# Hourglass attention plus token mixing on one core: query and key loaded as six rows on each of 96 partitions, value halves swapped while cast, four-quadrant products, explicit PSUM slots

## The chip, the cores and the metric

The kernel runs on one core of one Trainium2 chip. The metric is the device time of the whole kernel in microseconds (us), as the median of several runs. Medians and ranges that I quote are of all runs. Engines in the profile: PE is TensorE (matmul), PEld its weight loads, DVE VectorE, ACT ScalarE, POOL GpSimd, SPq the queue from which SyncE issues DMAs.

## The reference

```python
# q, k, v: (8, 8, 576, 64) = batch, heads, tokens, head width; float32
q_d, k_d, v_d = means over 4 consecutive tokens            # 144 coarse tokens
out_d     = softmax(q_d k_d^T / 8) v_d, each row repeated 4 times
out_local = softmax(q k^T / 8 where |i - j| < 4) v         # banded
x = (out_up + out_local) as (8, 576, 512)
wq, wk = x @ w_q, x @ w_k                                  # 512 x 64
mixed  = (wq wk^T / 8) @ x                                 # over tokens, no softmax
out    = relu(mixed) @ w_out                               # 512 x 512
```

## The kernel before

All eight batches run through a software pipeline: an ordered list of stages, with batches one or two apart interleaved. The helper `_InOrder` keeps every engine's instructions in program order. `...` marks cuts.

```python
def load_qk(b):
    q32 = big.tile([128, H, 4 * D], FP32, ...)      # 4 tokens on each of 128 partitions
    ...                                             # k32 alike
    r32 = big.tile([128, H, D], FP32, ...)          # the 64 tokens that remain, of q and of k
    for src, t in ((q[b], q32), (k[b], k32)):
        sp.dma_start(t, _ap(src, 0, [[4 * D, 128], [S * D, H], [1, 4 * D]]))       # 1024-byte pieces
    for i, src in enumerate((q[b], k[b])):
        sp.dma_start(r32[64 * i:64 * i + 64], _ap(src, 512 * D, [[D, 64], [S * D, H], [1, D]]))  # 256-byte pieces
def load_v(b):
    ...                                             # 10 loads, each 64 tokens on 64 partitions
    for n in range(NW):                             # 5 pairs of windows
        for c in range(2):
            sp.dma_start(v32[64 * c:64 * c + 64, n], _ap(v[b], K0[2 * n + c] * D, [[D, 64], [S * D, H], [1, D]]))
...
# casts of batch b > 0, all on GpSimd
pool.tensor_copy(...)                               # q, k, remainder
pool.tensor_copy(v16[:, :, :, 0:64], v32)           # values, one instruction of 2560 elements
...
def rem():                                          # transposed remainder to the end of qT and kT
    for i, t_ in enumerate((qT, kT)):
        evac("rem", t_[:, :, 512:S], _ap(pr, 64 * i, [[row(pr), 128], [128, NP], [1, 64]]))   # contiguous, VectorE
def sums():                                         # coarse q, k: GpSimd adds; for batch 0 the keys on VectorE
    add = (dve if i == 1 and b == 0 else pool).tensor_tensor
    ...
def av(n):                                          # value product of window pair n: two of four quadrants
    for s_ in range(2):
        for hh in range(NP):
            for c in range(2):
                h = 4 * (s_ ^ c) + hh
                pe.matmul(p_[64 * c:64 * c + 64, h // 4, 65 * hh:65 * hh + 65],
                          E[64 * c:64 * c + 64, h % 2, i, h // 2, :], v16[64 * c:64 * c + 64, n, h, :],
                          start=True, stop=True, tile_position=(64 * c, 64 * c))
def m2():                                           # second mixing product: seven matmuls of full width
    pe.matmul(p_, w_[NW][0:112], g["od"][0][0:112], start=True, stop=False)
    pe.matmul(p_, w_[NW + 1], g["od"][1], start=False, stop=False)
    for n in range(NW):
        pe.matmul(p_, w_[n], x[n], start=False, stop=(n == NW - 1))
    evac("M2", M2[0:64], p_[0:64], scale=s_mix)
def ol():                                           # output of the last 64 tokens, once per batch
    for r in range(4):
        pe.matmul(p_, rmx[:, r * S + 512:r * S + 640], wo16[:, r, :], start=(r == 0), stop=(r == 3))
```

The softmax here doesn't subtract the row's maximum and nothing guards it: scores larger than these inputs give would overflow.

## Time and profile before

| | before |
|---|---|
| time, median of 3 runs | 193.49 us (193.43 to 193.9) |
| span in the profile | 192.7 us |
| one batch in the steady part | 19.3 us |
| TensorE busy per batch | 18.5 us |
| first scores / first value product | 23.4 / 28.2 us |

The page of the profile gives busy time of each engine and then the span in 40 slices of 4.8 us: busy tenths, the granted TensorE clock, the busy share of the DMA engines, and what they moved.

```profile
PE 155.5 (81%) x2720; PEld 104.0 (54%) x2720; DVE 114.8 (60%) x286; ACT 110.7 (57%) x140; POOL 107.7 (56%) x122
...
PE   0034448885899989998999899989998999898790
...
PEclk9999555999789999999999999999999999999997
DMA  5999999899899799967999899969996943004215
GB/s 175 314 187 215 348 290 162 191 354 175 175 319 218 174 264 294 263 137 201 278 323 156 184 280 346 187 154 296 330 215 154 300 146 112 3 3 153 93 57 188
```

The next view cuts the steady part at the start of the token product (`pw`), once per batch. Its columns are the stretch, its length, each engine's busy time, the granted clock, the share of time that the DMA engines were busy, and GB/s.

```profile
core 0: us, PE busy (x) PEld busy (x) DVE busy (x) ACT busy (x) POOL busy (x), PEclk, DMA share, GB/s
62.36:81.66 19.30, 18.52 (x343) 12.43 (x341) 12.32 (x29) 13.23 (x18) 13.59 (x13) 1.00 0.95 247
81.66:100.96 19.30, 18.52 (x343) 12.43 (x341) 12.32 (x29) 13.17 (x18) 13.58 (x13) 1.00 0.87 234
```

TensorE is busy 96% of a batch at full clock. The DMA engines are busy 87 to 95% of it as well. The chain that ended last agrees with TensorE: this line gives its shares by engine.

```profile
PE 68%; DVE 17%; ACT 7%; issue 4%; POOL 2%; ACTq 0%; DVEq 0%
```

In the start, the same chain in order of time (start, length, what) shows the key sums of the first batch on VectorE, 9 us long:

```profile
18.22 1.37 DVE sum_296 L27
19.61 5.71 DVE kd_127 L27 x4
25.32 1.88 DVE kdt_129 L27
27.20 0.68 DVE vblk_201 L27 x2
```

Two groups of instructions are the remainder copies, and one batch's value cast. Columns: line, engine, operation, out and in, shapes, count, busy us and mean ns, idle time before them.

```profile
L27 DVE COPY qT<-pr 128x256 f16<-128x256 f16 x8 | 2.3, 292 | 5.1 <-PE pr L27 5.1
L27 POOL CAST v_1_149<-v_255 128x2560 f16<-128x2560 f32 x1 | 2.3, 2323 | 8.6 <-DMA v_255<-in_v_dram 8.6
```

### The profile page before, as it was taken

The page shows a single profiled execution, that of the slowest core. Times are in us where ns is not written, and L with a number is a line of the kernel's source. Part 1 is how long each engine was busy: PE and PEld are TensorE (multiplying, and loading weights), DVE is VectorE, ACT ScalarE, POOL GpSimd, SP SyncE. Part 2 cuts the span into 40 slices and gives each one's busy share as a digit, 9 for nine tenths or more (in the row PEclk, how much of TensorE's full clock was granted, in tenths as well). Part 3 has the DMA queues.
Part 4 walks back from the last instruction along what each step waited for, and adds up shares of the span by engine and source line. Part 5 has one row for each costly group of instructions (what it writes and reads, how often), then busy time and mean ns, then how long its engine had stood idle before and what let it go on. Part 6 is the DMA issues. An engine that isn't in the chain of part 4 may idle for free.

```text
span 192.7 us, 6374 instructions
## 1 busy us (share of the span) xinstructions
PE 155.5 (81%) x2720; PEld 104.0 (54%) x2720; DVE 114.8 (60%) x286; ACT 110.7 (57%) x140; POOL 107.7 (56%) x122
## 2 busy tenths in 40 slices
PE   0034448885899989998999899989998999898790
PEld 0034227853576647664776476647764776465330
DVE  6263978754646566656665666566656665685220
ACT  2037134954565767576757675767576757633422
POOL 5701991099748991895479547954895476000000
PEclk9999555999789999999999999999999999999997
DMA  5999999899899799967999899969996943004215
GB/s 175 314 187 215 348 290 162 191 354 175 175 319 218 174 264 294 263 137 201 278 323 156 184 280 346 187 154 296 330 215 154 300 146 112 3 3 153 93 57 188
DMA packets 74027, 40.54 MB, mean 210 GB/s; under 512 B 52432, under 2 KB 68880, under 8 KB 74000
## 3 DMA queue, kind: packets, MB, share of 16 engines
q1 hardware_dynamic: 73920, 40.12, 81.7%
q8 instruction: 21, 0.34, 0.7%
q14 instruction: 6, 0.05, 0.1%
q10 hardware_dynamic: 80, 0.03, 0.1%
HBM read 30.67 MB, written 9.44 MB: 208 GB/s over the span
## 4 chain that ended last, share of the span: by engine, by line
PE 68%; DVE 17%; ACT 7%; issue 4%; POOL 2%; ACTq 0%; DVEq 0%
PE po L27 15%; PE psc L27 6%; PE pav L27 5%; PE pw L27 4%; PE px L27 4%; PE pca L27 4%; PE pol L27 4%; DVE kd_127 L27 3%; PE pv L27 2%; PE pcs L27 2%; ACT kT L27 2%; PE pod L27 2%; DVE rz L27 1%; PE pws L27 1%; PE pwd L27 1%
## 5 line engine op out<-in xcount | busy, mean ns | idle before, releaser
L27 ACT COPY os<-po 128x1024 f32<-128x1024 f32 x16 | 16.2, 1012 | 14.7 <-issue 8.3
L27 DVE RECIPROCAL rz<-pav 128x8 f32<-128x8 f32 x40 | 8.1, 204 | 13.4 <-PE pav L27 13.4
L27 PE MATMUL po<-wo_91,rmx_227 128*128 128x512 f16 x64 | 15.3, 379 | 0.6 <-ACT rmx_227 L27 0.6
L27 PE MATMUL po<-wo_91,rmx_212 128*128 128x512 f16 x64 | 15.1, 379 | 0.0
L27 DVE COPY xT<-px 128x928 f16<-128x928 f16 (+1 forms) x32 | 13.8, 451 | 0.6
L27 PE MATMUL pq_236<-id_67,q_229 128*128 128x128 f16 x16 | 1.9, 312 | 12.6 <-DVE q_229 L27 12.6
L27 PE MATMUL psc<-id_67,neg 64*128 64x232 f16 (+1 forms) x80 | 9.4, 278 | 2.8 <-DVE vblk_201 L27 2.8
L27 PEld LDWEIGHTS <-rmx_227 128*128 128x128 f16 x80 | 7.2, 98 | 8.1 <-ACT rmx_227 L27 0.7
L27 PE MATMUL psc<-qT,kT 64*64 64x58 f16 (+1 forms) x640 | 11.4, 198 | 0.0
L27 PEld LDWEIGHTS <-rmx_212 128*128 128x128 f16 x80 | 7.2, 98 | 6.6
L27 DVE RECIPROCAL rc<-pca 128x8 f32<-128x8 f32 (+1 forms) x16 | 3.4, 211 | 11.8 <-PE pca L27 11.8
L27 PEld LDWEIGHTS <-wqk_90 128*128 128x128 f16 x96 | 8.3, 98 | 3.7 <-issue 0.9
L27 PEld LDWEIGHTS <-kT 64*64 64x64 f16 x640 | 8.7, 113 | 2.1 <-issue 2.1
L27 ACT COPY odT<-pod 128x448 f16<-128x448 f16 (+1 forms) x16 | 5.6, 402 | 6.3 <-PE pod L27 6.3
L27 PE MATMUL pw<-xT,wqk_90 128*128 128x288 f16 x64 | 9.2, 286 | 0.0
L27 PEld LDWEIGHTS <-q_229 128*128 128x128 f16 x16 | 1.6, 146 | 12.6 <-DVE q_229 L27 12.6
L27 POOL CAST v_0_147<-v_79 128x2560 f16<-128x2560 f32 x1 | 3.1, 3129 | 9.3 <-DMA w_92<-in_moe_w_k_dram 9.3
L27 DVE TENSOR_TENSOR wT_219<-pw,wTd 128x576 f16<-128x576 f32 x4 | 3.0, 758 | 8.6 <-ACT wTd L27 8.6
L27 DVE COPY ol<-pol 64x512 f32<-64x512 f32 x8 | 5.5, 682 | 4.3 <-PE pol L27 4.3
L27 DVE TENSOR_TENSOR wT_204<-pw,wTd 128x576 f16<-128x576 f32 x4 | 3.0, 758 | 8.0 <-ACT wTd L27 6.6
L27 DVE TENSOR_SCALAR rmx_227<-pmx 128x1024 f16<-128x1024 f32 x4 | 4.9, 1224 | 4.1 <-PE pmx L27 4.1
L27 POOL CAST v_1_149<-v_255 128x2560 f16<-128x2560 f32 x1 | 2.3, 2323 | 8.6 <-DMA v_255<-in_v_dram 8.6
(542 smaller groups left out, 540.9 us busy)
## 6 DMA issues: line engine op xcount, KB each, us to landing
out_dram<-os SPq DMA_DIRECT2D x16, 512.0 KB, 4.4
v_79<-in_v_dram SPq DMA_DIRECT2D x10, 128.0 KB, 4.6
v_255<-in_v_dram SPq DMA_DIRECT2D x10, 128.0 KB, 5.4
v_583<-in_v_dram SPq DMA_DIRECT2D x10, 128.0 KB, 3.5
v_1024<-in_v_dram SPq DMA_DIRECT2D x10, 128.0 KB, 4.4
v_1497<-in_v_dram SPq DMA_DIRECT2D x10, 128.0 KB, 3.6
v_1970<-in_v_dram SPq DMA_DIRECT2D x10, 128.0 KB, 4.3
v_2443<-in_v_dram SPq DMA_DIRECT2D x10, 128.0 KB, 3.4
```

The costliest lines, as they stand in the source:

```text
L27: return lambda *a, **k: self._tc.keep_in_program_order(f_(*a, **k))
```

## The change

Its intent: fewer and larger DMA pieces and no remainder loads; less TensorE work; value casts off GpSimd; a shorter start. Cut to its core:

```diff
-    q32, k32: [128, H, 4 * D] + r32: [128, H, D]; two loads of 1024-byte pieces, two of 256-byte pieces
+    t = big.tile([96, H, 6 * D], FP32, tag="in32", bufs=3)
+    sp.dma_start(t[:, lo:hi], _ap((q, k)[i][b], lo * S * D, [[6 * D, 96], [S * D, hi - lo], [1, 6 * D]]))
     ... (ten value loads as before, but issued one by one between other stages)

-    pool.tensor_copy(v16[:, :, :, 0:64], v32)
+    evac("va", v16[:, :, 0:4, 0:64], v32[:, :, 0:4])                       # VectorE for b > 0
+    for c in range(2):                                                     # heads 4..7: halves swapped
+        evac("vb%d" % c, v16[64 - 64 * c:128 - 64 * c, :, 4:8, 0:64], v32[64 * c:64 * c + 64, :, 4:8])

-    evac("rem", t_[:, :, 512:S], ...)                                      # 64 tokens, contiguous
+    evac("rem", t_.rearrange("p j (t f) -> p j t f", f=6)[:, :, :, 5], ...)  # 96 tokens, every sixth column

     value product (av):
-    h = 4 * (s_ ^ c) + hh
-    ... tile_position=(64 * c, 64 * c)
+    h, o = 4 * s_ + hh, 64 * (c ^ s_)
+    ... tile_position=(o, 64 * c)

     second mixing product (m2):
-    7 matmuls into p_[128 rows], one after the other
+    for i, (w_, x_) in enumerate(l_):
+        c = i % 2
+        pe.matmul(p_[64 * c:64 * c + 64], w_, x_, ..., tile_position=(0, 64 * c))
+    act.copy(half, p_[64:128])
+    dve.tensor_tensor(M2[0:64], p_[0:64], half, op=ALU.add)

+    the last 64 tokens of two batches share one output product (rest)
+    first batch: loads and casts in halves, q and k casts on ScalarE, coarse sums on TensorE (sums0)
+    constants are set between stages of the first batch instead of ahead of them
-    ps2 = tile_pool(bufs=3, PSUM); ps1 = tile_pool(bufs=2, PSUM)
+    free = {2: [0, 1, 2], 1: [3, 4]}                                       # slots given out explicitly
+    new order lists FIRST and ORDER
```

## The prediction

> **What bounds it now.** Between 43 and 160 us the kernel repeats every 19.3 us, once per batch (table of busy time by stage). TensorE is busy 18.5 of 19.3 us at full granted clock; ScalarE 13.2, VectorE 12.3, GpSimd 13.6, DMA share 0.72-0.97. The chain of waits is mostly TensorE (68% of the span), so TensorE's program order is the limit. Three costs surround it: a start of about 20 us before the repeated pattern (first scores at 23.4 us, but VectorE holds the chain to 27.9 us with the key sums: 1.37 + 5.71 + 1.88 us, and the query cast starts at 11.5 us behind constants); a granted clock of 0.66-0.68 from 20 to 41 us; and a last batch of 16.4 us after its token product starts.
>
> **What changes per batch on TensorE** (lengths from start to start in the timeline):
> - The value product uses two of four quadrants: 16 products in 0.37 us, while 32 score products on four quadrants take 0.38 us. Four-quadrant order should bring it to about 0.20 us; five windows save 0.85 us. [...]
> - The second mixing product: 7 x 0.23 = 1.62 us becomes four column pairs, about 0.87 us; saves 0.75.
> - The 64 remaining output rows: 0.86 us once per two batches; saves 0.43.
> - Transposes: 36 of 128 columns become 48 of 96, equal columns; about nothing. Split masks +0.05.
> - TensorE waits of some 0.8 us (0.4 before the mixing product, 0.2-0.3 before coarse products): new order and explicit PSUM slots perhaps halve them.
>
> Together 19.3 becomes about 16.9 us, nearly all on the critical path: 8 x 2.4 = 19 us.
>
> **What moves.** GpSimd loses the 2.3 us value cast and 0.6 us remainder cast, pays 2 x 2.85 instead of 2 x 1.9 us for query and key casts (96 partitions, 1.5 times the elements): about 12.8 us. VectorE gets the value cast, three pieces of about 0.75 us (the first 2048-element query cast took 1.19 us there), +0.65 for the halves' sum, loses 1.2 for a relu and 0.7 for the small output: about 14.3. ScalarE about 14.3. [...] Nothing should exceed TensorE, though all come near 85%.
>
> **DMA.** 1024 remainder pieces of 256 bytes per batch and two issues of about 1.5 us disappear, pieces grow from 1024 to 1536 bytes. Estimated from rates in the trace (about 180 GB/s on value loads, 400 on long pieces): about 17 us per batch becomes 16. Just under TensorE.
>
> **Start.** Split half-loads, casts on ScalarE, sums on TensorE, constants deferred: the VectorE key sums leave the chain. Batches 0 and 1 arrive in order; I expect some 8 us saved, the rest stays limited by the loads and the lower clock.
>
> **Prediction.** 193.5 - 19 - 8 = 166 us, range 157 to 175. Faster by over 2%: 0.97; within: 0.02; slower: 0.01.
>
> **What would show it.** Period 16.4-17.4 us in the middle; 16 value products in about 0.2 us; mixing product 0.9 us; small output four times in all; TensorE over 95% busy in the middle; first scores before 20 us; no VectorE key sums; DMA packets under 512 bytes down by 8192.
>
> **What would make it wrong.** Four-quadrant products not overlapping; value casts on VectorE blocked behind GpSimd so VectorE sets the period (then 172-180); DMA at its limit with 96 partitions (period stays near 18); the low-clock phase longer; or an order that removes all waits and a shorter start (below 157).

19 us from the batches and 8 us from the start lead from 193.5 to 166 us. The 0.20 us for the four-quadrant value product is my estimate from the 0.37 and 0.38 us that the trace shows. That casts on VectorE might be blocked behind GpSimd was not shown by any line of the trace before; it stands in the text as a risk alone.

## More of the kernel before

A run counts as fast or slow by its time and its granted TensorE clock.

The inputs of the attention are drawn with a scale of 0.1, so the scores are tiny. That matters for the experiments: several of them put tokens in wrong places on purpose, and the comparison with the reference still calls their output correct.

## The result, and the profile after

The changed kernel took 218.27 us (median of 4 runs, 216.34 to 221.26), the kernel before 193.46 us beside it (192.74 to 193.9). The ratio of the fast runs is 1.125 (95% interval 1.116 to 1.135). A ratio here is the mean time of one kernel's fast runs over the mean time of the other's fast runs of the same rounds, so it is not quite the ratio of the medians that I quote. The change made the kernel 12.5% slower. The profiled run was a fast one, with a span of 216.9 us.

The same lines of the page after the change:

```profile
PE 165.3 (76%) x2920; PEld 113.8 (52%) x2920; DVE 153.6 (71%) x312; ACT 119.0 (55%) x145; POOL 102.2 (47%) x106
...
PE   0467679669993997698868798669669979789691
...
PEclk9999555875996699999996799997995899799999
DMA  6999997899899989999799799989992021202215
GB/s 163 253 201 219 229 183 162 279 224 211 173 230 221 171 207 241 216 211 252 190 222 270 221 237 233 302 218 240 258 265 82 3 78 74 97 3 90 104 39 206
```

The steady part, cut at the token product again:

```profile
core 0: us, PE busy (x) PEld busy (x) DVE busy (x) ACT busy (x) POOL busy (x), PEclk, DMA share, GB/s
63.62:88.89 25.27, 19.57 (x362) 13.43 (x363) 20.90 (x36) 13.42 (x18) 14.39 (x9) 0.86 1.03 212
88.89:110.08 21.19, 17.25 (x360) 12.09 (x358) 18.67 (x34) 13.14 (x18) 12.35 (x7) 1.00 1.01 219
110.08:135.59 25.51, 20.25 (x364) 13.09 (x362) 18.85 (x34) 13.98 (x19) 12.40 (x7) 0.87 1.00 237
135.59:158.97 23.38, 18.20 (x360) 12.13 (x358) 18.64 (x34) 13.35 (x18) 12.36 (x7) 0.93 1.06 254
```

And the chain by engine:

```profile
PE 35%; DVE 25%; SPq 23%; DMA 5%; ACT 5%; issue 5%; DVEq 0%; ACTq 0%
```

What the reader is to see: a batch takes 21.2 to 25.5 us instead of 19.3. TensorE at full clock needs 17.25 us of it (before 18.52), so part of the saved work is real. But VectorE went from 12.3 to about 18.7 us, the DMA share is at 1.00 or above all the time, and their chain shares grew to 25% and 23%, while TensorE fell to 35%. The highest slices of the GB/s row before (346 to 354) are gone. The granted clock is also lower in places (0.86, 0.87 and 0.93). A batch is longer at full clock as well (88.89 to 110.08, 21.19 us), so the clock is not the whole of it; what it adds in the other stretches, where TensorE is busy for up to 20.25 us, no run separates. Between fast runs of one kernel it decided little: after_vpool, below, took 208.9, 211.0 and 210.7 us at mean clocks of 0.953, 0.915 and 0.897.

Two changes on VectorE stand out in the list of groups:

```profile
L27 DVE COPY qT<-pr 128x384 f16<-128x384 f16 x8 | 11.6, 1449 | 6.7 <-PE pr L27 6.7
L27 DVE COPY kT<-pr 128x384 f16<-128x384 f16 x8 | 12.7, 1589 | 0.0
L27 DVE CAST v_2_101<-v_2137 64x1280 f16<-64x1280 f32 x2 | 3.7, 1873 | 0.0
```

The remainder copies take five times as long for 1.5 times the elements. The value cast has three pieces; the line shows the two on half the partitions, 1.87 us on average: one took 0.95 us, the other 2.79. The timeline of VectorE (start, length, what) shows the three pieces as one row of 4.75 us:

```profile
132.96 0.95 DVE L27 COPY xT<-px_2666 128x928 f16<-128x928 f16 x2
133.94 4.75 DVE L27 CAST v_2_101<-v_2137 128x1280 f16<-128x1280 f32 x3
```

At the same moment, GpSimd (same view) sits 2.40 us ahead of its next addition without any wait that the profile knows, runs it for 2.11 us, and only then do the casts end:

```profile
132.22 1.15 POOL L27 TENSOR_TENSOR qd<-sum_2896 128x576 f16<-128x576 f32 x1
135.77 2.11 POOL L27 TENSOR_TENSOR sum_2899<-kT 128x1152 f32<-128x1152 f16 x1 [2.40 <-issue]
137.96 1.29 POOL L27 TENSOR_TENSOR kd_87<-sum_2899 128x464 f16<-128x464 f32 x1
```

The two pieces on 64 partitions have the same shape: the second of the three took 0.95 us (134.93 to 135.88 us), the third 2.79 (135.90 to 138.69). GpSimd's addition began at 135.77 us, as the second piece ended, and ended at 137.88 us; the third piece ended 0.81 us after it. By these times the addition waited for the first two pieces and the third piece for the addition. That is a reading of this trace; the whole row took 4.75 us here and 2.89 us with GpSimd idle (forms, below).

### The profile page after: what moved, and what is told of

The parts are those of the page before. It is cut to its first block, busy times and chain, and to the rows that moved or that the text cites. A ratio compares the mean times of both kernels' runs of the same rounds, so it can differ in the third digit from the quotient of the medians.

```text
span 216.9 us, 6753 instructions
## 1 busy us (share of the span) xinstructions
PE 165.3 (76%) x2920; PEld 113.8 (52%) x2920; DVE 153.6 (71%) x312; ACT 119.0 (55%) x145; POOL 102.2 (47%) x106
## 4 chain that ended last, share of the span: by engine, by line
PE 35%; DVE 25%; SPq 23%; DMA 5%; ACT 5%; issue 5%; DVEq 0%; ACTq 0%
SPq L27 23%; DVE v_1_100 L27 6%; DVE v_2_101 L27 4%; DMA out_dram<-os 3%; DVE qT L27 3%; DVE kT L27 2%; DMA v_493<-in_v_dram 2%; DVE v_0_99 L27 2%; PE pv L27 2%; PE pol L27 2%; DVE xT L27 1%; ACT half L27 1%; PE pws L27 1%; PE pw L27 1%; PE pod L27 1%
## 5 line engine op out<-in xcount | busy, mean ns | idle before, releaser
L27 DVE COPY qT<-pr 128x384 f16<-128x384 f16 x8 | 11.6, 1449 | 6.7 <-PE pr L27 6.7
L27 DVE COPY kT<-pr 128x384 f16<-128x384 f16 x8 | 12.7, 1589 | 0.0
L27 ACT CAST vd_1_92<-pv 128x512 f16<-128x512 f32 x4 | 2.4, 588 | 14.4 <-PE pv L27 14.4
L27 PEld LDWEIGHTS <-wqk_69 128*128 128x128 f16 x96 | 8.2, 98 | 3.0 <-DVE xT L27 0.3
L27 PEld LDWEIGHTS <-rmx_98 128*128 128x128 f16 x64 | 6.8, 114 | 5.6 <-ACT rmx_98 L27 0.4
L27 PEld LDWEIGHTS <-rmx_86 128*128 128x128 f16 x64 | 6.7, 113 | 4.9
L27 ACT CAST vd_0_80<-pv 128x512 f16<-128x512 f32 x4 | 2.4, 588 | 12.4 <-PE pv L27 12.4
L27 PEld LDWEIGHTS <-q_145 96*128 96x128 f16 x48 | 4.6, 141 | 8.6 <-ACT q_145 L27 8.6
L27 PEld LDWEIGHTS <-P_103 128*32 128x32 f16 x48 | 1.5, 97 | 13.9 <-issue 13.9
L27 PEld LDWEIGHTS <-neg 64*128 64x128 f16 x112 | 4.1, 103 | 4.9 <-issue 4.2
L27 POOL TENSOR_TENSOR sum_2896<-qT 128x1152 f32<-128x1152 f16 x1 | 2.1, 2104 | 9.6 <-ACT qT L27 9.6
L27 POOL TENSOR_TENSOR sum_3859<-qT 128x1152 f32<-128x1152 f16 x1 | 2.1, 2104 | 8.6 <-ACT qT L27 8.6
L27 POOL TENSOR_TENSOR sum_3381<-qT 128x1152 f32<-128x1152 f16 x1 | 2.1, 2107 | 8.2 <-ACT qT L27 8.2
L27 PEld LDWEIGHTS <-k_148 96*128 96x128 f16 x48 | 4.8, 141 | 1.8 <-issue 1.8
L27 ACT CAST q_145<-q_111 96x1536 f16<-96x1536 f32 x2 | 2.9, 1471 | 4.3 <-DMA q_111<-in_q_dram 4.3
L27 POOL TENSOR_TENSOR sum_2407<-qT 128x1152 f32<-128x1152 f16 x1 | 2.1, 2107 | 6.7 <-DVE rc L27 6.7
L27 DVE CAST v_2_101<-v_973 64x1280 f16<-64x1280 f32 (+1 forms) x3 | 5.0, 1660 | 0.1
```

The lines of the kernel that those rows point to most:

```text
L27: return lambda *a, **k: self._tc.keep_in_program_order(f_(*a, **k))
```

## The experiments

The theory after reading the two traces: three new costs reach the critical path. (a) Loads on 96 partitions run at a lower rate. (b) Value casts on VectorE take long and collide with GpSimd. (c) The remainder copies write at a step of six elements. The rivals: one of them alone explains it; or the new order of stages and the PSUM slots do; or the TensorE savings are not there at all.

### Costs measured by themselves (forms)

A kernel with only loads of several forms, one pair after the other, and then copies and casts of several forms. Its output is wrong, and it ran once.

> No attention is computed here, the output is wrong on purpose. It measures the disputed costs by themselves. Loads: if 96 partitions of 1536-byte pieces are slow in themselves (theory DMA), the phase moves about 225 GB/s against about 390 for 128 partitions of 1024 bytes; 96 partitions of 1024 bytes and 128 partitions of 1536 bytes tell whether the number of partitions or the size of the piece does it. If the loads were slow only because of what ran beside them, all phases but the 256-byte one reach 350 or more. VectorE forms: the 384-element copy out of PSUM takes about 0.45 us when written without gaps and 1.45 to 1.6 us at a step of 6 if the step is the cause. Value casts: about 0.95 us a piece on VectorE with GpSimd idle; 2 us or more for a piece that meets a running GpSimd cast, if the two block each other.

For each form, the stretch between two landings gives its rate. The view by stretch shows, in this order, 128 partitions with 1024-byte pieces, 96 with 1536, 96 with 1024, 128 with 1536, and 64 with 2304 (read the last two columns, DMA share and GB/s):

```profile
6.13:9.61 3.48, 0.00 (x0) 0.00 (x0) 3.41 (x3) 0.20 (x2) 0.00 (x0) 1.00 1.10 319
9.61:14.72 5.11, 0.00 (x0) 0.00 (x0) 4.58 (x4) 0.19 (x1) 0.00 (x0) 1.00 1.10 228
19.93:23.27 3.34, 0.00 (x0) 0.00 (x0) 3.28 (x3) 0.20 (x2) 2.50 (x2) 1.00 1.12 235
26.53:29.03 2.50, 0.00 (x0) 0.00 (x0) 0.00 (x0) 0.20 (x1) 2.44 (x2) 1.00 1.03 326
32.25:38.06 5.81, 0.00 (x0) 0.00 (x0) 0.00 (x0) 0.20 (x1) 1.75 (x1) 1.00 1.03 217
```

| form of one load | bytes per partition | time |
|---|---|---|
| 128 partitions x 8 pieces of 1024 B | 8 KB | 2.9 to 3.5 us |
| 96 x 8 of 1024 B | 8 KB | 3.3 us |
| 128 x 5 of 1536 B | 7.5 KB | 2.5 to 3.2 us |
| 96 x 8 of 1536 B (the change) | 12 KB | 5.1 to 5.2 us |
| 96 x 8 of 1536 B, partitions 32 to 127 | 12 KB | 5.1 us |
| 96 x one piece of 12288 B | 12 KB | 4.4 to 4.8 us |
| 64 x 8 of 2304 B | 18 KB | 5.8 to 6.2 us |

The piece size matters little in this range: 12 KB in one piece took 4.4 to 4.8 us where eight pieces of 1536 B took 5.1. What the rate went with is the number of partitions: in eight pieces each, 96 moved 228 to 238 GB/s, hardly more than 64 (196 to 217), and 128, in eight or five, moved 319 to 345 (from the stretches above, or a pair's bytes over the time between its landings). The DMA engines read as busy throughout in all five stretches, at 1.03 to 1.12: this share cannot tell a slow transfer from a fast one. The bytes on each partition do not give the time alone either: 8 KB took 3.3 us on 96 partitions and 2.9 to 3.5 on 128, but 12 KB on each of 96 took 5.1 us where 18 KB on each of 64 took 5.8 to 6.2. Why the rate goes with the partitions is not shown; the runs show only the times.

An estimate of one batch's query and key loads from these rates: before, 16 KB per partition in the two main loads and 2 + 2 KB in the remainders, about 8 us at the 0.36 to 0.44 us per KB of the table's first row; after, 24 KB in two loads of 5.1 us, about 10.2 us. The ten value loads, 64 partitions each, are the same in both.

The rest of this run: 384 elements from PSUM on VectorE, in f16, took 0.36 us at write step 1, 0.58 at step 2, 1.01 at step 4, 1.43 at step 6 and 1.85 at step 8: about 0.21 us more per further element of step, and none of these steps was free. ScalarE took 0.46 to 0.48 us at step 1 and 1.44 at step 6, so moving such a copy there is no cure. The three value cast pieces took 2.89 us together with GpSimd idle (first row of VectorE's timeline) and 3.60 with GpSimd beginning the same casts behind it (second row; its third piece took 1.62, less than the 2 us that I expected):

```profile
84.50 2.89 DVE L27 CAST v<-f 128x1280 f16<-128x1280 f32 x3
...
19.69 3.60 DVE L27 CAST v<-f 128x1280 f16<-128x1280 f32 x3
```

### Each cost taken out alone (after_vpool, after_remact, after_load128)

```diff
 after_vpool:    "va": "d", "vb0": "d", "vb1": "d"  ->  "p", "p", "p"      # value casts on GpSimd
 after_remact:   "rem": "d"  ->  "a"                                      # step-6 copies on ScalarE
 after_load128:  # 128 partitions x 1024 B and one load of the remaining 128 KB as 128 x 1024 B; tokens misplaced on purpose
+    sp.dma_start(w[:, 256 * lo:256 * hi], _ap(src, lo * S * D, [[4 * D, 128], [S * D, hi - lo], [1, 4 * D]]))
+    sp.dma_start(w[:, 2048:2304], _ap(src, 512 * D, [[S * D, H], [4 * D, 16], [1, 4 * D]]))
```

> The changed kernel with the three value casts given back to GpSimd. Theory VectorE (blocked casts set the period): VectorE loses 4.7 us a batch, the wait before the value means goes, and the time falls from 218 to about 200. Theory DMA (the 96-partition loads set it): GpSimd and VectorE get freer, but the loads stay at about 220 GB/s, and the time stays above 210.

> The changed kernel with the two strided copies of every sixth row moved from VectorE to ScalarE. Theory VectorE: 3 us a batch leave VectorE, and as ScalarE has 6 to 8 us free per batch, the time falls by about 10 us, to 208. Theory DMA: within 3 us of 218. If ScalarE pays more than 1.5 us for such a copy too, it may get slower.

> The changed kernel with the same bytes of q and k loaded as 1024-byte pieces on 128 partitions; the values land in the wrong places, so the result is wrong on purpose, the instructions of all engines stay as they are. Theory DMA: loads at 350 GB/s or more, the start about 6 us shorter, the period near 19.5, so about 197. Theory VectorE: only the start gains, the time stays above 210.

Measured: 210.8 us (ratio to before 1.083, 1.076 to 1.089), 214.5 us (1.094, 1.086 to 1.101) and 218.1 us (one fast run at 211.3; the other three, at 217.8 to 220.6, count as slow, so there is no ratio). The first two gain a little; for the third the runs leave anything from nothing to 6 us. Taken alone, this would nearly acquit the loads. It does not: two limits stand close to each other, and freeing one leaves the other. From 60 to 160 us VectorE is busy 86% in after_load128 (waits for GpSimd within an instruction included), and the DMA share is 1.00 in after_vpool.

### The costs taken out together (after_flat_vpool, after_flat_vpool_load128)

In these, the step-6 copies write contiguously. That puts tokens in the wrong columns; the work is otherwise the same. The same edit (not shown) also makes ScalarE's copies of the other five rows contiguous; these took 1.76 us instead of 1.77.

```diff
-    evac("rem", t_.rearrange("p j (t f) -> p j t f", f=6)[:, :, :, 5],
+    evac("rem", t_[:, :, 480:S],
```

> The changed kernel with both VectorE costs out of it: value casts on GpSimd, and the rows of q and k left in the order of the transposes, so that no copy is written at a step of six (the token order, and with it the local window, is wrong on purpose; all instructions and sizes stay). The loads stay on 96 partitions. Theory VectorE: VectorE falls below 12 us a batch, so TensorE sets the period: 17 to 18 us, about 180 in all. Theory DMA: 10.3 us for q and k at 230 GB/s, 7.3 for values, 3 for the output, so 20.6 us a batch until the loads end near 165 us: 200 or more.

> As after_flat_vpool, and the q and k bytes loaded on 128 partitions (wrong result on purpose). If the two VectorE costs and the loads together are the whole loss, this gives what the prediction expected of the rest of the change: 170 to 180 us. If it stays above 190, something else in the change costs as much, such as the order of the steps or the lower granted clock.

Measured: 209.6 us (ratio 1.074, 1.065 to 1.082) with (b) and (c) out, and 191.4 us (0.989, 0.983 to 0.995) with all three out. The group line confirms that the edit did what it should (0.354 us per copy instead of 1.449), and that the casts went to GpSimd:

```profile
L27 DVE COPY qT<-pr 128x384 f16<-128x384 f16 x8 | 2.8, 354 | 7.2 <-PE pr L27 7.2
L27 POOL CAST v<-v 64x1280 f16<-64x1280 f32 (+1 forms) x23 | 28.9, 1255 | 20.7 <-DMA v<-in_v_dram 17.0 <-DMA w<-in_moe_w_q_dram 2.9
```

So the three costs account for the whole loss against the kernel before and a little more: 218.3 down to 191.4 us. All the rest of the change, new order and PSUM slots included, stays in this kernel, so the order by itself is not what made it slower. The expected 170 to 180 us were missed all the same: the rest of the change brings next to nothing of the forecast gain.

### Each cost left in alone (after_flat_load128, after_vpool_load128)

> The changed kernel without strided copies and with loads on 128 partitions, value casts still on VectorE (wrong on purpose). With after_flat_vpool_load128 at 191 it prices the value casts: 195 if VectorE at about 16 us a batch is no limit any more; 203 or more if the casts that block and are blocked hold the value means and TensorE behind them.

> The changed kernel with value casts on GpSimd and 128-partition loads (token placement wrong on purpose), so that of its three costs only the six-element-step writes of the remainder copies are left. Beside the kernel with all three taken out (191.4 us): if the step writes cost VectorE their 2.4 us per batch and VectorE is then on the chain, 198 to 210 us; if they hide behind TensorE and the loads, within 2 us of 191.4.

With only the value casts on VectorE left in: 215.0 us (1.104, 1.095 to 1.113). With only the step-6 copies: 198.1 us (1.018, 1.008 to 1.027; the expectation was 198 to 210 or a tie with 191.4). With only the loads on 96 partitions: 209.6 us, from above. The table uses the means of the fast runs.

| cost | removed alone from 217.6 | left in alone, above 191.3 |
|---|---|---|
| value casts on VectorE | -7.4 us | +23.1 us |
| loads on 96 partitions | -6.3 us (one fast run; the slow ones show about 0) | +16.3 us |
| step-6 copies (first column: moved to ScalarE, not cured) | -5.3 us | +6.1 us |

Some of the differences are between different rounds. The right column adds up to 45.5 us where all three together cost 26.3: the costs overlap. Whichever is removed last gets the credit, which is why the left column says so little.

The trace of after_flat_load128 (a slow run) says how much of the casts' length is waiting: about 5.8 us a batch (22 pieces, of 1.69 and 2.00 us on average) where three undisturbed pieces take 2.89. No run has the casts on VectorE without GpSimd work beside them, so how the 23 us divide between the work and the collision is not shown.

### Only the loads, in the kernel before (before_load96, before_load96b, before_ctl128)

The rival for the loads is that the 128-partition edit helps for some other reason. So the kernel before got the loads of the change and nothing else (its remainder casts read from the same tile; tokens misplaced).

> The kernel before with only the loads of the change: q and k as six rows on each of 96 partitions, no loads of remainder rows (wrong result on purpose, all other work unchanged). Theory DMA: DMA needs 20.6 us a batch against a period of 19.3, so the loads lag and the time rises to 200 to 206. If loads were no limit: 193 or a little less, as two issues of 1.5 us a batch go.

This run was spoiled, and its 217.3 us say nothing: I gave the loads three buffers in turn without moving the second batch's load. So its keys were loaded over the first batch's queries before these were cast, and the first query cast waited for them until 32.4 us. Mended, with a control of the same buffers and 128 partitions:

```diff
 before_load96b:  sp.dma_start(t[0:96], _ap(src, 0, [[6 * D, 96], [S * D, H], [1, 6 * D]]))
 before_ctl128:   sp.dma_start(w[:, 0:2048], _ap(src, 0, [[4 * D, 128], [S * D, H], [1, 4 * D]]))
                  sp.dma_start(w[:, 2048:2304], _ap(src, 512 * D, [[S * D, H], [4 * D, 16], [1, 4 * D]]))
 both: in32 of three buffers; loads of batch 1 and of w_out after the first casts
 only before_load96b: fill(0), fill(1), fill(2)      # ScalarE clears the unused rows, 2.3 us each
```

> before_load96 was spoiled by its own buffers: the first query cast waited to 33.7 us for the third buffer's reload. Here the second batch's loads stand after that cast, as they should. Again the kernel before with only the 96-partition loads (wrong result on purpose). Theory DMA: a period between 19.3 and 20.6 us where loads run, a start some us later than before because 2.36 MB come at 230 instead of 345 GB/s twice: 198 to 206 in all, above before_ctl128 of the same call by 5 or more. If the loads are no limit under this order: equal to before_ctl128 within 2 us.

> The control of before_load96b: the same three buffers, order and bytes, but 1024-byte pieces on 128 partitions (values in the wrong places, wrong on purpose). It should stand within 2 us of 193; if it too is slower, the three buffers cost the time and not the 96 partitions.

Measured: 212.7 us (ratio 1.094, 1.086 to 1.101) against 199.4 us for the control (1.025, 1.016 to 1.033). The steady part by stretch, for the 96 partitions:

```profile
80.00:160.00 80.00, 74.07 (x1273) 49.26 (x1273) 46.55 (x110) 50.57 (x66) 50.47 (x46) 0.96 1.05 222
```

and for the control:

```profile
80.00:160.00 80.00, 76.89 (x1401) 51.88 (x1399) 51.44 (x123) 55.17 (x70) 53.47 (x48) 1.00 0.93 231
```

The two differ by 13 us, but not by the loads alone: only the 96-partition kernel has the three fills, and the last of them stands on ScalarE between the first casts and copies of the start. Where the fills play no part, from the token product of the second batch to that of the eighth, six periods take 122.5 us against 113.9: these 8.6 us are the loads'. The instruction counts of the stretch tell the same: in 80 us TensorE got 1273 matmuls done against 1401. The control was to stand within 2 us of 193 and did not; its 6 us over before are not explained.

In these six periods TensorE stands still for 5.3 us in four gaps for which the profile names no wait ("issue"); the control has none there. One of them:

```profile
97.72 0.58 PE L27 MATMUL pm<-od,wk 128*128 128x512 f16 x1 [2.05 <-issue]
```

Each ends 1.4 to 1.7 us after a load of 16 KB on the instruction queue (q8 of the page, read from the packets of the trace) has ended. The same holds, at 1.3 to 1.7 us, for all 50 such gaps over 0.3 us that the profiles of the 18 whole kernels show; after_flat_vpool has 13.9 us of them, after_flat_vpool_load128 5.1 us. The kernel before has 21 of these loads for 5440 matmuls and weight loads, the kernel after 23 for 5840, 254 to 259 to a load; from that I estimate that they bring TensorE's own instructions, and read the gaps as instructions that come late while the DMA engines are full. The timing is shown; what the loads carry is not, and no run moves them, so the cause is a reading.

### The TensorE savings, in the kernel before (before_trim, before_trim_order)

The column pairs of `m2` and the paired last 64 tokens were put into the kernel before. In the second kernel the mixing products were moved behind other products, to give the new evacuation time.

```diff
 before_trim_order:  ..., (0, "av1"), (-1, "mx0"), (0, "av2"), (0, "cs0"), (-1, "mx1"), (0, "cs1"), ...
                 ->  ..., (0, "cs0"), (0, "av1"), (0, "av2"), (-1, "mx0"), (0, "cs1"), ..., (-1, "mx1"), ...
```

> The kernel before with only two TensorE savings of the change: the second mixing product on two column halves, and the 64 last rows of two batches in one product. TensorE bound: 0.75 plus 0.43 us a batch, so 184 to 187; the halves' sum on VectorE comes before the next product, which may give up to 0.7 us a batch back, so 190. If TensorE were not the limit, 193.

> before_trim gained nothing, although TensorE lost about 0.8 of 20 us busy: its waits before the mixing product, the coarse products and the last value product grew to 1.6 us a batch. Theory PSUM slots: those steps stand in one row and each waits for an evacuation of about 1 us by ScalarE; with the mixing products moved behind the value and coarse products the waits go and the period falls to 18.2 us: about 186. If TensorE work were really all that counted and the slots no matter: unchanged at 195.

Measured: 195.2 us (ratio 1.006, 0.998 to 1.013) and 196.0 us (1.011, 1.004 to 1.018). Both are nominally slower than before, although TensorE's busy time in 80 us of the steady part fell from 76.89 to 73.55 us (before_trim). The waits of the same 80 us show where it went. Of the kernel before:

```profile
PE pmx L27 <- ACT E_1_145 L27: 0.8, 2, 0.4
PE pmx L27 <- ACT E_0_135 L27: 0.8, 2, 0.4
```

Of before_trim (columns: who waited for whom, us in total, times, longest):

```profile
PE pmx L27 <- DVE M L27: 1.9, 3, 0.6
PE pcs L27 <- ACT rmx L27: 1.4, 3, 0.5
PE pav L27 <- ACT Ec L27: 0.8, 4, 0.2
```

The mixing product is shorter, but its result now passes through two instructions (0.58 us on ScalarE, 0.68 on VectorE) before the next product can start, and the products behind it wait for PSUM slots to be emptied. My reading was that in that stretch the evacuation by ScalarE and VectorE sets the pace, and that the long mixing product had been covering it. Its test missed: before_trim_order, which moves the mixing products away, was expected at about 186 us and took 196.0; TensorE then waited 3.6 us of the 80 for VectorE at the value products instead. So what holds these two kernels is not shown. Here 96% busy (18.5 of 19.3 us) did not mean that less TensorE work makes the kernel faster.

The four-quadrant value product itself gains only when two of its kind stand together. This timeline of the changed kernel has a pair back to back, 0.15 us apart, then the first matmuls of `m2`:

```profile
141.11 0.32 PE L27 MATMUL pav_2853<-v_2_101,E_1_89 64*64 64x65 f16 x16
141.26 0.30 PE L27 MATMUL pav_2875<-v_2_101,E_1_89 64*64 64x65 f16 x16
141.49 0.40 PE L27 MATMUL pm_2903<-od_2560,wk_83 112*64 112x512 f16 x1
```

The other three of a batch stand alone between other products and take 0.36 us until the next product starts (145.57 to 145.93 us), as long as the two-quadrant form before (0.38 us, 104.69 to 105.07). Why a group that stands alone takes longer is not shown. `m2` took 0.98 us until the next start at full clock (1.62 before, 0.87 predicted).

### The start (before_wo, before_sums, before_start, before_start2)

The last open piece was the 8 us that I had expected from the start. In the kernel before, the first batch's sums were moved to TensorE (before_sums), the second batch's value loads were put ahead of the output weights (before_wo), and both (before_start). All of these compute the right result.

```diff
 before_wo:    load_qk(1); + load_v(1); wo loads
 before_sums:  "sums": sums  ->  sums0 if b == 0 else sums
+    pe.matmul(p_[i][:, j // 2, o:o + 128], t_[:, f, 2 * j:2 * j + 2, :], id16, start=(f == 0), stop=(f == 3))
+    pe.matmul(p_[i][:, j // 2, o + 128:o + T], r16[64 * i:64 * i + 64, 2 * j:2 * j + 2, :], S4[...], ...)
```

> The kernel before with the second batch's value loads issued ahead of the output weights. If the loads alone bound the start: 1 to 4 us faster than before (190 to 192.5 us). If VectorE's key sums bound the start, the values land some 3 us sooner and the time stays within 1 us of before.

> The kernel before with the first batch's sums on TensorE, load order untouched. VectorE's 9 us of key sums leave the chain and the first value product comes about 3 to 4 us sooner (24.5 us instead of 28.2). If the late values of the second batch then hold TensorE (their cast ends at 40.4 us), the time gains under 1.5 us; if not, 3 to 4 us.

> Both edits to the start of the kernel before. Theory: two limits near each other, so together 3 to 5 us (188 to 190.5 us), more than the sum of each alone. Rival: the start is given back later to loads, and both together stay within 1.5 us of before.

Measured: 196.4 us (1.010, 1.003 to 1.018), 193.2 us (0.994, 0.986 to 1.001) and 197.1 us (1.017, 1.011 to 1.023). My theory of two limits missed. The sums do bring the first value product from 28.2 to 23.1 us (24.5 expected). But putting the output weights last made a new wait in both kernels that have it: their cast stands ahead of the first batch's last evacuations in ScalarE's program order, and waited 5.1 us for them. The waits of before_start from 30 to 45 us:

```profile
ACT wo L27 <- DMA wo<-in_moe_w_out_dram: 5.5, 2, 5.1
```

So the cast was moved one turn later:

```diff
-    ..., (0, "score1"),                         # casts of wqk and wo both at (0, "weights")
+    ..., (0, "score1"), (-1, "weights_o"),      # the cast of wo here
```

> The two edits to the start with the cast of the output weights one turn later, so that ScalarE no longer waits for it. Theory: the early start is kept, the first token product comes at about 35.5 us (39.8 before) and the time falls by 3 to 5 us, to 188.5 to 191. Rival: the loads set the pace after an early start, the second period is longer than 22.5 us and the time stays within 1.5 us of before.

Measured: 192.6 us (191.4 to 195.6, ratio 0.989, 0.984 to 0.994, six runs against eleven of before). That is 1.1% faster than the kernel before, and less than I expected. In the profile the first token product came at 38.1 us (39.8 before, 35.5 expected), and the token product of the second batch came 4.5 us earlier (57.9 against 62.4 us), so about 2 us reach the end and the rest is given back later. That profile fell in a slow run, where one later batch took 24.4 us instead of 19.3. Its values landed late, but TensorE did not wait for them: it stood still once, for 3.5 us until 1.3 us after an instruction load, and at a granted clock of 0.86 it was busy 2.4 us longer. Whether the fast runs lose their part there too is open. before_start2 is the best correct kernel.

## Why the prediction was wrong

1. "TensorE's program order is the limit" and "nearly all on the critical path": failed. The saved TensorE work exists (18.5 to 17.25 us per batch at full clock), but in the kernel before two of its three parts were worth nothing (before_trim, 195.2 us). TensorE was busy, but its work alone did not set the time; what did is a reading (evacuation) whose test missed.
2. "three pieces of about 0.75 us" for the value cast: mis-sized. The three together, 2.25 us by that, took 2.89 us undisturbed and 4.4 to 5.0 us in the kernel. I named the collision with GpSimd as a risk and gave it no microseconds in the sum. Left in alone, the casts cost 23 us over the seven batches that have them.
3. "about 17 us per batch becomes 16" for the DMAs: wrong in sign. I costed bytes and piece sizes with a rate of 400 GB/s "on long pieces" (the trace before has 388 in its best slice of 1.25 us); what the rate went with was the number of partitions. Query and key loads went from about 8 to 10.2 us, and the whole from about 17 (a mean share of 0.89 in five batches of 19.3 us) to 20.6 us, an estimate from the rates of the first experiment. The values' 180 GB/s, which I had read in the trace and put down to short pieces, belong to loads of 64 partitions, and with pieces of 2304 bytes 64 partitions gave only 196 to 217. The loads on 96 partitions cost 9 to 13 us in the kernel before and 16 us in the changed one.
4. The remainder copies at step six: not in the sum at all. I carried "transposes: about nothing" and overlooked what follows them. They are 1.45 + 1.59 us per batch instead of 0.29 + 0.28, and cost 6.1 us where they are the only one of the three left.
5. "VectorE about 14.3 us" followed from 2 and 4: it was 18.6 to 20.9.
6. "some 8 us saved" in the start: failed. The token product of the first batch began at 45.9 us instead of 39.8, 6 us later. With the three costs out it began at 43.0 us, and the start as a whole gained 3 us by the second batch (59.1 against 62.4). The best start that I built gains 4.5 us at that point.
7. Right or nearly so: 0.98 us for `m2`, where 0.87 was predicted; four small outputs instead of eight; 8431 fewer packets under 512 bytes (8192 predicted); first scores earlier (22.6 us, though not under 20); four-quadrant products at 0.15 to 0.23 us, but only when two stand together.
8. The list of risks contained the cause. "Value casts blocked behind GpSimd" and "DMA at its limit with 96 partitions" both happened; the error was to treat them as alternatives with 172 to 180 us each, when a batch that is near three limits can lose on all at once. The chance of 0.01 for slower was not earned by anything in the profile.

What stays open: the kernel with the three costs out runs at 191.4 us, 25 us above the prediction. Points 1 and 6 name where most of the expected gain was not there to be had, but I did not divide these 25 us by experiment. It is also not the forecast kernel free of costs: its value casts keep GpSimd about 3.8 us a batch, where the single cast before took 2.3.

## What to carry to other kernels

Cost a load by the rate measured for its number of partitions (here 196 to 217 GB/s for 64, 228 to 238 for 96 and 319 to 345 for 128), not by its bytes or its piece size: 1.18 MB on 64 partitions in pieces of 2304 B took 5.8 to 6.2 us here, on 96 in pieces of 1536 B 5.1. When TensorE and the DMA engines stand as high as here (96% and 87 to 95% of a batch before the change), price each moved instruction in its new place with its real access pattern and its real neighbour (a write step, 0.36 against 1.43 us here; a cast beside a running GpSimd, 0.95 against 2.79). And test removals in combination: with limits this close, taking out one cause alone showed at most 5 to 7 us for causes worth 6 to 23.
